# A sequence layer and an expert layer on one core: the same pieces of work, issued in another order

## The chip, the cores and the metric

The kernel runs on one core of a Trainium2 chip. The core has five engines that each take their own instructions strictly in the order in which the program issued them: TensorE (PE in the profile, with PEld for its weight loads), VectorE (DVE), ScalarE (ACT), GpSimd (POOL) and SyncE (SP, whose queue starts nearly all transfers). An instruction whose inputs are not there yet holds up everything behind it on its engine. The metric is the device time of one execution in microseconds (us); lower is better.

## The reference

Two residual layers run one behind the other, on 2048 positions of 512 channels, in float32:

```python
x = A_u                                  # 1 x 2048 x 512
h = x + S4D(layernorm(x))                # long convolution, one kernel of 2048 taps a channel
h2 = h + PEER(layernorm(h))              # 32 heads, each picks one of 256 experts

# S4D: 128 complex modes a channel
dt = exp(log_dt); A = -exp(log_A_real) + 1j * A_imag; C = (C_real + 1j * C_imag) * dt
K = 2 * Re(sum over the modes of C * exp(A * dt * position))       # 512 x 2048
y = irfft(rfft(u) * rfft(K)) + u * D_skip

# PEER: K = 1, so the softmax over the chosen ones is 1
s1 = q1 . k1 (16 scores), s2 = q2 . k2 (16 scores) for each position and head
expert = 16 * argmax(s1) + argmax(s2)
out = sum over the heads of gelu(xf . u[expert]) * v[expert]
```

## The kernel before, in words

**How the order is made.** The function does not issue instructions while it walks through the computation. It builds a `Plan`: `plan.add(engine, cost, fn, r=, w=, t=, ...)` records a piece of work as a closure, with the keys that it reads and writes, and numbers the pieces 0 to 1727 as they are added. At the end of the function `plan.run(ORDER)` calls the closures in the order of a table of 1728 numbers written at the top of the file; it only asserts that each piece's predecessors have run. A closure issues one instruction or many. So the table alone decides which instruction stands behind which on every engine, and in which order the transfers stand in SP's queue. Tiles come from small rings of buffers, and the first writer of a tile waits until the readers of the tile that had the buffer before are through: two buffers each for the tables `mg`, `pg` and `gf`, seven PSUM banks shared by most of the first phase, two and four PSUM tiles in the second, two for the raw weights `wq`.

**First phase, the convolution.** The 512 channels are treated as four blocks of 128 (the digit behind u, k, U, T, ia in the names), and the taps of each channel are produced by 32 *tables* (tab0 to tab31, eight for each block), 16 channels a table.
- The parameters are loaded and worked up once by ACT and DVE: decays `E0` (for tables 0 to 15) and `e1` (for tables 16 to 31, stored to DRAM and read back later) by 11 exponentials each in `decays` (L373), a root (L354), an arctangent (L355), the phase tables `RS0` and `A0` on DVE (L315 to L342, L364).
- A table: POOL makes the phases `pg` (L557) and the magnitudes `mg` (L588, its tails L594) out of the powers `TS` (L570 to L581) and the steps `PS` (L538 to L550); ACT takes sines and cosines (L644, L645, L647); DVE multiplies them (L651 to L664) into `gf` and `mg`; PE sums over the modes with 64 small matmuls into `kps` (L690), from which `k` is copied.
- Eight groups of weights w0 to w7 are folded from the query weights `wq` and the expert keys on PE (L828, L836) with ACT copies between (L832, L840) and stored to `w_d` (L844). They fill gaps of the first phase.
- The input is loaded twice, once for the statistics of the layernorm (`x`, L273; DVE statistics L232, PE sums L242 and L255, ACT root L262), once for the data (`xs`, L502; normalised on DVE at L505 and L508).
- The transform: stage 1 on PE (`s1u`, `s1k`, L471), ACT copies (L474), stage 2 (`s2yu`, `s2yk`, L488), the product of the spectra on DVE (L732 to L735, for block 3 with POOL's L743), the first stage back (`ia`, L764), copies to `T` (L772, L777), stores to `t_d` in DRAM (L789).

**Second phase, the experts.** The folded weights come back as `w_q` (L921), split into `w_hi` (ACT, L924) and `w_lo` (DVE, L925). Eight blocks of 256 positions follow, each as: the last stage back (`ib`, L1036) and the residual `h` on DVE (L1043), the layernorm's mean and centred values (PE L1093 and L1105, DVE L1073 and L1080, ACT L1076 and L1083), the variance (POOL L1060, PE L1124, ACT root L1128), scores `sc` (L1150), `xu` (L1157), the top of each head (DVE `mx` L1176, `eq` L1181, `kq` L1186; POOL `ks` L1192 and L1194; DVE `ei` L1199, `ix` L1202), the gelu (ACT L1206), the gather as a one-hot product (PE `ta` L1227, `ixt` L1242, `bc` L1258; ACT L1231, L1246, L1262; DVE compares `oh` L1280; PE `cnt` L1290; DVE `actT` L1299, ACT `whi` L1302, DVE `wlo` L1305), the sum over the experts (PE `o` L1327, for the last block L1324) and the residual (DVE `ob` L1332, store L1337). The last block is cut into two halves of 128 positions.

Of the kernel before, what the change touches and what calls it, by code (L numbers as in the profile page):

```python
# [27 lines left out]
def view(t, off, dims):  # L28
# [6 lines left out]
    16, 0, 2, 1, 17, 18, 4, 23, 80, 3, 5, 9, 7, 24, 65, 19, 26, 20, 180, 21, 22, 10, 34, 6, 183, 35, 36, 197, 29, 185,  # L35
    28, 58, 25, 31, 37, 39, 70, 40, 75, 41, 247, 32, 60, 30, 66, 67, 143, 983, 113, 12, 68, 244, 118, 42, 38, 44, 86,
    33, 61, 91, 114, 117, 120, 101, 43, 107, 119, 150, 11, 46, 27, 45, 53, 71, 47, 54, 76, 988, 77, 78, 48, 63, 55, 184,
    72, 73, 181, 74, 79, 87, 88, 81, 69, 82, 83, 92, 93, 84, 182, 198, 94, 187, 49, 50, 51, 189, 52, 62, 188, 96, 89,
    186, 190, 90, 191, 102, 103, 104, 196, 984, 248, 192, 193, 194, 56, 57, 64, 85, 199, 200, 993, 214, 105, 201, 202,
    985, 95, 195, 59, 215, 203, 245, 986, 97, 98, 8, 204, 99, 205, 100, 106, 108, 109, 110, 217, 206, 218, 216, 121,  # L40
    219, 220, 207, 221, 222, 223, 14, 994, 995, 127, 987, 224, 226, 229, 989, 990, 13, 126, 227, 231, 136, 208, 230,
    999, 123, 991, 992, 228, 232, 125, 209, 111, 1004, 225, 233, 1000, 234, 1009, 235, 1001, 236, 1002, 1003, 996, 1005,
    246, 997, 1006, 1007, 251, 253, 128, 998, 124, 1008, 255, 389, 237, 238, 257, 122, 210, 211, 115, 1014, 212, 213,
    15, 239, 116, 129, 249, 1010, 1020, 252, 250, 130, 1011, 1012, 1015, 254, 112, 131, 260, 263, 132, 133, 1013, 265,
    1025, 258, 1016, 1017, 242, 261, 256, 240, 134, 151, 1018, 262, 266, 267, 241, 269, 259, 135, 137, 138, 139, 141,
    264, 243, 278, 281, 140, 283, 152, 155, 142, 157, 270, 268, 386, 279, 280, 285, 156, 144, 282, 153, 154, 271, 1021,
    287, 1022, 1026, 1027, 290, 145, 284, 272, 293, 148, 286, 1028, 146, 149, 349, 1029, 158, 273, 295, 1023, 147, 297,
# [1401 lines left out]
```

## Time and profile before

| what | us |
|---|---|
| runs of the kernel before | 504.03, 503.99, 502.99 (median 503.99) |
| span of the profiled execution, first to last instruction | 503.2 |
| time of the profiled execution beside its span | not recorded apart; the three runs lie -0.2 to +0.8 about the span |
| PE busy, of the span | 449.0 (89%) |
| DVE busy | 407.8 (81%) |
| POOL busy | 325.5 (65%) |
| ACT busy | 298.3 (59%) |
| mean granted TensorE clock | 0.986 |

A row of the timeline reads: start, duration, engine, line, operation, output and inputs by the program's names, shapes, count; in square brackets the idle time of the engine just before the row, and what ended it. A row of the windows gives one stretch of the span: for each engine its busy time with the number of instructions in brackets, then the granted clock, the share of the 16 DMA engines, and what they moved. The profile's line numbers are those of the kernel before; in the kernel after each line stands one lower, since the table takes one line of text more.

### The profile page before, as it was taken

Reading aid. Unit: us, or ns where it says so; the run is one execution under the profiler, and the core shown is the slowest. Engines: PE = TensorE matmul, PEld = TensorE weight load, DVE = VectorE, ACT = ScalarE, POOL = GpSimd, SP = SyncE. Lnnn points to the kernel's source line nnn. Section 1 sums busy time; section 2 is a strip of 40 time slices with the busy share of each in tenths; the row PEclk is TensorE's granted clock in tenths of the full one; section 3 lists DMA queues with packets and bytes.
Section 4 is the critical chain, followed back from the end, with each engine's and each line's share of the span. In section 5 each row is a group of like instructions: output and inputs, shape, how many; then the busy total and the mean of one; then the engine's idle time right before and its main releaser. Section 6 shows DMA issues by size and latency. Waiting matters only on the chain.

```text
span 503.2 us, 16702 instructions
## 1 busy us (share of the span) xinstructions
PE 449.0 (89%) x7206; PEld 390.3 (78%) x7206; DVE 407.8 (81%) x708; ACT 298.3 (59%) x594; POOL 325.5 (65%) x344
## 2 busy tenths in 40 slices
PE   0266879999998999999998889999999999999985
PEld 0144568888997999889997787877878888787874
DVE  5998998899968998899745574888979686978984
ACT  4867799967987588967965362644043430416230
POOL 4989989999999999997824303572163516536130
PEclk9998799999999999999999899999999999999999
DMA  8959474234033300631017689310171311010012
GB/s 253 403 198 381 143 288 148 66 86 179 2 111 124 85 3 1 212 126 45 1 61 259 200 275 283 127 61 1 57 227 55 109 63 43 1 44 0 1 68 62
DMA packets 27362, 61.05 MB, mean 121 GB/s; under 512 B 7028, under 2 KB 14456, under 8 KB 26136
## 3 DMA queue, kind: packets, MB, share of 16 engines
q1 hardware_dynamic: 27136, 59.85, 34.9%
q8 instruction: 57, 0.93, 0.7%
q10 hardware_dynamic: 152, 0.13, 0.1%
q14 instruction: 17, 0.14, 0.1%
HBM read 46.08 MB, written 13.89 MB: 119 GB/s over the span
## 4 chain that ended last, share of the span: by engine, by line
PE 50%; DVE 22%; ACT 10%; POOL 10%; issue 4%; DMA 3%; SPq 1%; ACTq 0%; DVEq 0%; POOLq 0%
PE sc L1150 12%; PE ia L764 9%; DVE oh L1280 5%; PE s2yk L488 3%; PE xu L1157 3%; PE kps L690 3%; PE s2yu L488 3%; POOL pg L557 3%; PE s1u L471 3%; DVE st L232 2%; PE o L1327 2%; PE ib L1036 2%; PE cnt L1290 2%; ACT t L645 2%; POOL mg L594 2%
## 5 line engine op out<-in xcount | busy, mean ns | idle before, releaser
L557 POOL TENSOR_TENSOR pg<-PS 128x1024 int32<-128x1024 int32 x32 | 68.8, 2150 | 0.5
L588 POOL TENSOR_TENSOR mg<-TS 128x1024 f32<-128x1024 f32 x32 | 62.6, 1958 | 7.2 <-PE kps L690 4.5
L1280 DVE TENSOR_SCALAR oh<-idxb,ec_s 128x2048 bf16<-128x2048 bf16 (+1 forms) x72 | 50.3, 757 | 6.8 <-ACT idxb L1262 6.8
L764 PE MATMUL ia<-ca_s,U 128*128 128x128 f32 x256 | 50.6, 280 | 0.4 <-POOL U L743 0.4
L1060 POOL TENSOR_TENSOR vs<-hc 128x256 f32<-128x256 f32 x8 | 7.0, 872 | 62.6 <-ACT hc L1083 62.6
L1192 POOL TENSOR_TENSOR ks<-kq 128x512 f32<-128x512 bf16 x16 | 17.2, 1078 | 45.9 <-DVE kq L1186 44.8
L645 ACT ACTIVATE t<-t,halfpi 128x512 f32<-128x512 f32 x64 | 42.4, 662 | 2.1
L1150 PE MATMUL sc<-w_hi,hhi 128*128 128x480 f32 x128 | 42.4, 412 | 0.0
L644 ACT ACTIVATE t<-pg 128x512 f32<-128x512 int32 x64 | 38.9, 609 | 3.2 <-DVE gf L652 2.2
L764 PEld LDWEIGHTS ia<-ca_s,U 128*128 128x128 f32 x256 | 39.8, 196 | 0.6 <-POOL U L743 0.6
L647 ACT ACTIVATE t<-pg 128x512 f32<-128x512 int32 x64 | 38.2, 608 | 2.8 <-POOL pg L557 1.5
L764 PE MATMUL ia<-ca_s,yk 128*128 128x128 f32 x192 | 38.1, 280 | 0.4 <-DVE mg L664 0.4
L1150 PE MATMUL sc<-w_lo,hhi 128*128 128x480 f32 x128 | 38.4, 380 | 0.0
L1150 PE MATMUL sc<-w_hi,hlo 128*128 128x480 f32 x128 | 38.3, 380 | 0.0
L594 POOL TENSOR_TENSOR mg<-TS 128x512 f32<-128x512 f32 x32 | 37.4, 1170 | 0.4
L690 PE MATMUL kps<-mg 128*32 128x64 f32 x1024 | 34.0, 230 | 3.8 <-DVE mg L664 2.2
L488 PE MATMUL s2yk<-yk,c_s 128*128 128x128 f32 x256 | 34.7, 282 | 1.1 <-ACT yk L474 0.7
L471 PE MATMUL s1u<-c_s,xs 128*64 128x128 f32 x512 | 33.3, 277 | 2.5 <-DVE xs L508 1.6
L690 PE MATMUL kps<-gf 128*32 128x64 f32 x1024 | 33.7, 229 | 1.8 <-issue 1.8
L488 PEld LDWEIGHTS s2yk<-yk,c_s 128*128 128x128 f32 x256 | 30.6, 191 | 4.2 <-issue 1.4
L488 PE MATMUL s2yu<-yu,c_s 128*128 128x128 f32 x256 | 32.6, 279 | 0.3
L471 PEld LDWEIGHTS s1u<-c_s,xs 128*64 128x64 f32 x512 | 27.6, 137 | 5.4 <-DVE xs L508 1.7
(198 smaller groups left out, 1377.5 us busy)
## 6 DMA issues: line engine op xcount, KB each, us to landing
wq<-wq SPq DMA_DIRECT2D x25, 512.0 KB, 4.5
t_d<-T SPq DMA_DIRECT2D x24, 256.0 KB, 3.4
Tb<-t_d SPq DMA_DIRECT2D x8, 768.0 KB, 6.0
x<-xa SPq DMA_DIRECT2D x8, 512.0 KB, 5.6
xs<-xb SPq DMA_DIRECT2D x16, 256.0 KB, 5.3
xt<-xt SPq DMA_DIRECT2D x8, 512.0 KB, 4.8
out<-ob SPq DMA_DIRECT2D x7, 512.0 KB, 3.0
c_s<-wq SPq DMA_DIRECT2D x4, 512.0 KB, 8.3
```

Of the source, the lines that this page charges most:

```text
L471: T.matmul(ps[64 * k:64 * k + 64, g, :], lhs8(4 * n + g), c1_s[:, k], start=True, stop=True)
L488: T.matmul(ps[:, k, :], c2_s[:, kk, :], y[:, :, kk, :], start=True, stop=True)
L557: G.tensor_tensor(view(pg, 0, [[32, 2 * NC], [8, 4], [1, 8]]), view(t["PS"], 1024 + off, [[1, 2 * NC], [128, 4], [0, 8]]), view(t["PS"], 8 ...
L588: G.tensor_tensor(view(mg, 0, [[96, NC], [8, 8], [1, 8]]), view(ts, 512 + 8 * o, [[8, NC], [1, 8], [0, 8]]), view(ts, 8 * o, [[8, NC], [0, ...
L594: G.tensor_tensor(view(mg, 64, [[96, NC], [8, 4], [1, 8]]), view(ts, 1536 + o, [[1, NC], [64, 4], [0, 8]]), view(ts, 1024 + 8 * o, [[8, NC ...
L644: A.activation(p, pg[:, :, k], AF.Abs)
L645: A.activation(p, p, AF.Sin, scale=-SINSCALE, bias=halfpi)
L647: A.activation(p, pg[:, :, k], AF.Sin, scale=SINSCALE)
L690: T.matmul(kps[32 * q:32 * q + 32, 2 * g + h, :], m[:, d, 64:96], m[:, d, 0:64], start=(e == 0), stop=(e == 1))
L764: T.matmul(ps[:, g, :], t[:, 4 * n + g].rearrange("p a b -> p (a b)"), ca_s[:, s, :], start=(s == 0), stop=(s == 1))
L1150: T.matmul(ps[:, 512 * h:512 * h + 480], t[x_][:, q, ts], I[w_][:, q, 480 * h:480 * h + 480], start=(q == 0 and x_ == w_), stop=(q == 3 an ...
L1280: V.tensor_scalar(oh[:, :, 0:ln], t["idxb"][:, :, sl], S["ec"][:, 4 * e + j:4 * e + j + 1], None, op0=ALU.is_equal)
```

## The change

Only the table `ORDER` is another: the same 1728 numbers in another order. No piece of work, no tile, no ring, no shape and no engine of a piece differs. The first rows of the diff show how it looks:

```diff
@@ -32,87 +32,88 @@
 ORDER = (
-    16, 0, 2, 1, 17, 18, 4, 23, 80, 3, 5, 9, 7, 24, 65, 19, 26, 20, 180, 21, 22, 10, 34, 6, 183, 35, 36, 197, 29, 185,
...
```

The order differs nearly everywhere, on every engine. ACT gets four instructions more, 562 rows where there were 558: table loads, since the activation functions alternate more often (one pair around `e1`, one pair in the second phase). All other engines issue the same instructions. Three places follow in rows of the issue order; a name with a number behind it is one tile, and x11 stands for eleven instructions in a row.

**ACT in the first part of the program, before.** The eleven exponentials of `e1` stand between the two parts of `E0` and ahead of the arctangent (L355), on which the phases of the first table hang.

```order
L373 ACTIVATE E0_116<-pb_98 128x64 x11
L351 ACTIVATE par2_101<-pa_97 128x64
L353 ACTIVATE pb_98<-pa_97 128x64
L373 ACTIVATE e1_104<-pb_98 128x256 x11
L352 ACTIVATE pa_97<-pa_97 128x64
L373 ACTIVATE E0_116<-pb_98 128x192 x11
```

After, at the same place:

```order
L374 ACTIVATE E0_116<-pb_98 128x64 x11
L352 ACTIVATE par2_101<-pa_97 128x64
L354 ACTIVATE pb_98<-pa_97 128x64
L353 ACTIVATE pa_97<-pa_97 128x64
L374 ACTIVATE E0_116<-pb_98 128x192 x11
```

and 61 rows further down, behind the sines of table 3:

```order
L646 ACTIVATE t11_3_612<-t11_3_612,halfpi_62 128x512
L841 COPY wh2_551<-wps10_592 128x120
L833 COPY wt13_646<-wps13_633 128x128
L374 ACT_TABLE_LOAD
L374 ACTIVATE e1_104<-pb_98 128x256 x11
L833 COPY wt12_734<-wps12_693 128x128
L699 COPY k0_1_759<-kps0_1_648 128x512
L841 COPY wh3_771<-wps12_693 128x120
L648 ACT_TABLE_LOAD
L648 ACTIVATE t00_4_799<-pg4_773 128x512
```

What moved: `e1` out of the way of the arctangent, to a place where it costs a change of table there and back. On DVE, the statistics of the layernorm (L232), of which 24 stood before the first table's products, now all stand behind them; on PE the sums of the tables (`kps`) stand further back among the other matmuls throughout the first phase. SP issues `ka` and `kb` before three of the five parameters, and the last two of the eight loads of `x` behind the second store of folded weights.

**DVE at the turn from the first phase to the second, before.** The last copies of the first phase (`T3`) are followed by two splits of the query weights, and these by the residual of the first block, from which the mean is taken.

```order
L777 COPY T3_4229<-ia3_2_4319 64x64x4 x2
L777 COPY T3_4229<-ia3_4_4337 64x64x4 x2
L925 TENSOR_TENSOR w_lo_4193<-w_q1_4309,w_hi_4192 128x960
L925 TENSOR_TENSOR w_lo_4193<-w_q0_4312,w_hi_4192 128x960
L1043 TENSOR_TENSOR h0_4418<-ib0_0_4366,xt0_4316 128x4x128
L1043 TENSOR_TENSOR h0_4418<-ib0_1_4383,xt0_4316 128x4x128
```

After:

```order
L778 COPY T3_4257<-ia3_6_4298 64x64x4 x2
L778 COPY T3_4257<-ia3_5_4307 64x64x4 x2
L926 TENSOR_TENSOR w_lo_4196<-w_q0_4281,w_hi_4195 128x960
L948 CAST ident_b_4197<-ident_60 128x128
L949 MEMSET ones_d_4198 128x128
L1044 TENSOR_TENSOR h0_4415<-ib0_1_4363,xt0_4361 128x4x128
L1044 TENSOR_TENSOR h0_4415<-ib0_0_4380,xt0_4361 128x4x128
```

What moved: one of the two splits, that of `w_q1`, stands behind the centring of the first block now. A little earlier, in SP's queue, three of the last four loads of `wq` stand ahead of the stores of `T2` (L789) and the fourth between their two halves; before, all four stood behind all eight stores. On PE two of the four folds of w7 (`wps28`, `wps29`) now stand ahead of the last stage 2 of block 3 (`s2yk3`), and the other two ahead of its fifth and seventh part, each behind the wait for its own load; before, the four were spread from its fifth part to its end.

**DVE at the end, before.** `oh65` to `oh71` and `oh64` are the compares of the second half of the last block, `oh60` the last of the first half.

```order
L1280 TENSOR_SCALAR oh60_7147<-idxb7_6999,ec_s_4198 128x8x128
L1299 TENSOR_TENSOR actT7_7080<-cnt7_0_7105,actT7_7080 128x2x128
L1280 TENSOR_SCALAR oh65_7182<-idxb7_6999,ec_s_4198 128x8x128
L1280 TENSOR_SCALAR oh67_7184<-idxb7_6999,ec_s_4198 128x8x128
L1280 TENSOR_SCALAR oh66_7186<-idxb7_6999,ec_s_4198 128x8x128
L1280 TENSOR_SCALAR oh64_7188<-idxb7_6999,ec_s_4198 128x8x128
```

After:

```order
L1281 TENSOR_SCALAR oh60_7145<-idxb7_7006,ec_s_4201 128x8x128
L1281 TENSOR_SCALAR oh65_7148<-idxb7_7006,ec_s_4201 128x8x128
L1281 TENSOR_SCALAR oh64_7186<-idxb7_7006,ec_s_4201 128x8x128
L1281 TENSOR_SCALAR oh67_7188<-idxb7_7006,ec_s_4201 128x8x128
L1281 TENSOR_SCALAR oh66_7190<-idxb7_7006,ec_s_4201 128x8x128
L1300 TENSOR_TENSOR actT7_7079<-cnt7_0_7093,actT7_7079 128x2x128
```

What moved: four compares of the second half ahead of the product of the first half. On PE, both broadcasts `bc` of the second half and half of the first half's `cnt` stand ahead of its twelve `xu` matmuls (before: `xu` first), and the first half's `o` stands between the two halves of the second `cnt` (before: ahead of both).

162 rows, old and new, of the table ORDER are left out of this document.

## The prediction, as put on record before the changed kernel ran

> **What bounds the kernel now.** I read the page's first part, then the windows, then the timeline where the windows show TensorE idle.
>
> ```profile
> PE 449.0 (89%) x7206; PEld 390.3 (78%) x7206; DVE 407.8 (81%) x708; ACT 298.3 (59%) x594; POOL 325.5 (65%) x344
> ```
>
> PE is idle for 503.2 - 449.0 = 54.2 us; no order of the same matmuls can win more than that. Where it is idle, the windows say:
>
> ```profile
> 0.00:20.00 20.00, 2.05 (x29) 1.37 (x33) 13.87 (x41) 13.40 (x47) 12.27 (x24) 1.00 0.89 307
> 20.00:40.00 20.00, 11.82 (x195) 7.53 (x187) 19.08 (x51) 12.17 (x31) 17.54 (x22) 1.00 0.73 272
> 40.00:60.00 20.00, 13.86 (x314) 10.31 (x314) 18.66 (x61) 16.13 (x37) 19.61 (x18) 0.74 0.78 284
> 60.00:80.00 20.00, 16.66 (x417) 13.82 (x420) 18.99 (x35) 18.58 (x39) 18.12 (x16) 1.00 0.56 199
> 70.00:255.00 185.00, 180.28 (x3396) 166.54 (x3397) 162.74 (x268) 152.85 (x292) 173.66 (x158) 1.00 0.26 85
> 262.00:282.00 20.00, 16.47 (x267) 14.22 (x264) 11.99 (x20) 10.84 (x24) 10.11 (x8) 1.00 0.67 226
> 340.00:360.00 20.00, 20.00 (x195) 16.37 (x193) 18.07 (x28) 5.35 (x11) 3.72 (x4) 1.00 0.01 2
> 480.00:503.20 23.20, 16.09 (x270) 13.71 (x262) 14.85 (x29) 6.24 (x12) 2.97 (x4) 1.00 0.21 71
> ```
>
> The columns behind the length are PE, PEld, DVE, ACT and POOL. In the first 80 us PE is idle for 35.6 us while DVE is full from about 6 us on; from 70 to 255 PE is idle for only 4.7 us, with POOL close behind it (173.7 of 185); at the turn of the phases it loses 3.5 us in 20; in the second phase nothing; at the end 7.1. So a new order can win at the start (by getting DVE's work done sooner), at the turn, and at the end. In between it can only lose, or win the 4.7.
>
> **The start.** PE becomes full when the first stage 1 of the input can run, and this hangs on the last statistic of the layernorm on DVE:
>
> ```profile
> 11.49 3.48 ACT L373 ACTIVATE e<-pb 128x256 f32<-128x256 f32 x11 [1.11 <-DVE pb L359]
> 25.30 0.24 ACT L355 ACTIVATE pa<-pa 128x64 f32<-128x64 f32 x1
> 29.32 2.13 POOL L557 TENSOR_TENSOR pg<-PS 128x1024 int32<-128x1024 int32 x1
> 6.20:67.90 61.70, 33.20 (x664) 23.42 (x664) 57.93 (x162) 46.69 (x125) 56.25 (x60) 0.92 0.81 296
> 47.87 0.87 DVE L232 BATCH_NORM_STATS2 st<-x 128x6 f32<-128x128 f32 x4 [1.34 <-DMA x<-xa]
> 67.92 1.97 PE L471 MATMUL s1u<-c_s,xs 128*64 128x128 f32 x32 [1.58 <-DVE xs L508]
> ```
>
> Taking `e1` (3.48 us) from ACT's path, and 24 statistics from DVE's (four take 0.87, so 5.2), lets the arctangent at 25.30 and the first phases at 29.32 come some 3.5 to 5 us sooner, with the first tables behind them. But s1u does not wait for tables. It waits for DVE, and DVE does the same instructions ahead of it: of the 61.7 us up to s1u it is busy for 57.9. The most that an order can win is the 3.8 idle, of which 1.34 is the wait for x; the two last loads of x now stand behind one store more, so this wait can also grow. I take -0.3, with -3.8 and +2 as bounds. The two table loads around `e1`, with `e1` itself, are 3.5 + 2.6 = 6.1 us on ACT at its new place behind table 3. ACT has room there: 3.9 us idle in 40:60, and at least 3.5 by which its sines start sooner, 7.4 together. Uncovered the 6.1 would fall on the table chain.
>
> ```profile
> 18.88 0.57 ACT L352 ACTIVATE pa<-pa 128x448 f32<-128x448 f32 x1
> 19.48 1.28 ACT L354 ACT_TABLE_LOAD   x1
> 20.77 0.21 ACT L354 ACTIVATE par<-par 128x64 f32<-128x64 f32 x1
> ```
>
> A switch costs 1.28 here, since the instruction ahead ends at 19.45 and the next starts at 20.77. The Trainium skill speaks against this part of the change more strongly: "ScalarE: Activation LUTs", section "What ACT_TABLE_LOAD costs", counts a drain of about 1.38 us on top of 1.28 for every switch, 2.66 in all. By the page the pair and `e1` would be 3.5 + 5.3 = 8.8 us, 1.4 more than the room, and the forecast at most 1.4 us later. The trace does not agree: its row shows no drain, and the sum goes by the row.
>
> While s1u waits, PE works off one fold of weights more than before (34 matmul groups of L828 ahead of it, not 32), which is gone from the full stretch:
>
> ```profile
> 60.49 0.43 PE L828 MATMUL wps<-wq,ka_s 128*32 128x128 f32 x8 [0.42 <-DVE gf L652]
> 60.73 0.40 PE L828 MATMUL wps<-wq,kb_s 128*32 128x128 f32 x8
> 61.52 0.33 PE L836 MATMUL wps<-ident,wt 128*128 128x128 f32 x1 [0.39 <-ACT wt L832]
> ```
>
> 0.64 from the first start to the second end, and 0.33 less overlap: -0.9, or 0 if PE had a hole for it later anyway.
>
> **The full stretch.** Matmuls are the same. The order puts the sums of the tables (kps) later among them, so PE should wait less for DVE's tables, but POOL gets its two `mg` buffers back later:
>
> ```profile
> L588 POOL TENSOR_TENSOR mg<-TS 128x1024 f32<-128x1024 f32 x32 | 62.6, 1958 | 7.2 <-PE kps L690 4.5
> L690 PE MATMUL kps<-mg 128*32 128x64 f32 x1024 | 34.0, 230 | 3.8 <-DVE mg L664 2.2
> 156.88 0.26 PE L690 MATMUL kps<-gf 128*32 128x64 f32 x4 [1.78 <-issue]
> 254.08 1.16 POOL L594 TENSOR_TENSOR mg<-TS 128x512 f32<-128x512 f32 x1
> 262.07 0.32 PE L690 MATMUL kps<-mg 128*32 128x64 f32 x8
> ```
>
> POOL is through with table 31 at 255.24, and PE takes up its sum at 262.07; what ACT and DVE do between is 2 to 3 us, so some 4 us of delay on POOL stay unseen. I take 0. Bounds: -3.8, PE's waits for tables gone, and +5, a delay of 9 on POOL.
>
> **The turn.** Up to the first `ia` the pace is DVE's, then POOL's:
>
> ```profile
> 269.31 0.69 DVE L732 TENSOR_TENSOR yu<-s2yk,U 128x512 f32<-128x512 f32 x1 [5.28 <-ACT ki L739]
> 276.87 0.69 DVE L732 TENSOR_TENSOR yu<-s2yk,U 128x512 f32<-128x512 f32 x1 [0.36 <-ACT ki L739]
> 281.84 0.71 PE L764 MATMUL ia<-ca_s,U 128*128 128x128 f32 x2 [0.36 <-POOL U L743]
> ```
>
> One fold and two transposes more stand ahead of stage 2, about 1.0 us by the rows above; the new place of the four wq loads in SP's queue removes the late wq, for DVE 0.36. Together +0.6, between 0 and +1.3.
>
> Behind the last copy of T, two w_lo hold up `h`, the mean and so the scores:
>
> ```profile
> 299.51 2.23 DVE L925 TENSOR_TENSOR w_lo<-w_q,w_hi 128x960 fp32r<-128x960 f32 x2
> 301.77 1.29 DVE L1043 TENSOR_TENSOR h<-ib,xt 128x512 f32<-128x512 f32 x2
> 303.71 0.69 DVE L1073 TENSOR_TENSOR hc<-h,mean 128x512 f32<-128x512 f32 x1 [0.65 <-PE mean L1093]
> 305.21 0.68 DVE L1080 TENSOR_TENSOR hlo<-hc,hhi 128x512 fp32r<-128x512 f32 x1
> ```
>
> One leaves: -1.1; two small casts that came before now stand there: +0.4. One half's hlo now precedes the other half's hc, 0.6 sooner. Late next is the second half, which the first scores cover. Taken: -1.2; bounds -2 (the scores of the half that is ready start at once) and 0 (w_hi or x is late instead).
>
> **The second phase.** PE is full in 340:360, and no work changes. The two table loads more, 2.6 us, lie on an ACT that is busy for 5.35 of 20. 0, between -1.5 and +1.5.
>
> **The end.** DVE waits, then has eight compares left:
>
> ```profile
> 492.13 0.42 DVE L1299 TENSOR_TENSOR actT<-cnt,actT 128x256 f32<-128x256 f32 x1 [2.37 <-PE ta L1227]
> 492.47 3.25 DVE L1280 TENSOR_SCALAR oh<-idxb,ec_s 128x1024 bf16<-128x1024 bf16 x8
> 488.25 1.63 PE xu L1157 x12
> 496.97 2.07 PE o L1324 x16
> 499.06 0.69 DVE L1332 TENSOR_TENSOR ob<-o,h 128x512 f32<-128x512 f32 x1 [1.55 <-PE o L1324]
> ```
>
> Four compares, 1.6 us, move into the 2.37, which their inputs allow because `bc` no longer queues behind xu's 1.63. The last compare is then done about 1.6 sooner. But the first half's `o`, 2.07 long, now stands between the halves of the last `cnt` and ends later than the last compare; this gives some 0.3 back. -1.3, between -1.9 and 0.
>
> Sum: -0.3 - 0.9 + 0 + 0.6 - 1.2 + 0 - 1.3 = -3.1 against the span of 503.2: 500.1. The median of the runs lies 0.8 above that span, so **about 500.9 us**.
>
> **Rivals.** A measurement of this kernel tells 0.2% (1.0 us) from no change.
>
> *No change.* The gains at turn and end are 2.5 us together; a POOL delay of 6 (2 beyond the cover) cancels most. For it: the stretch in which PE has no slack is most of the span, and its order is shuffled throughout. Time: 503.2 to 504.5.
>
> *POOL becomes the bound: slower.* Place: POOL's L588 in the later tables. A kps that is late by one table on PE makes POOL stand; a table is 2.15 + 1.96 + 1.17 = 5.3 us of POOL by its rows (first row below; the others are quoted above and here). Two such stalls, 10.6, less the cover of 4, push the sum of table 31, the turn and all behind by 6.6; with -3.1 this is +3.5, about 507.5. It decides as soon as POOL's delay exceeds 4 + 3.1 = 7.1 us. For it: POOL has 11.3 us of idle time in 185. Against it: earlier tables at the start give it a lead of 3.5 to 5.
>
> ```profile
> L557 POOL TENSOR_TENSOR pg<-PS 128x1024 int32<-128x1024 int32 x32 | 68.8, 2150 | 0.5
> L594 POOL TENSOR_TENSOR mg<-TS 128x512 f32<-128x512 f32 x32 | 37.4, 1170 | 0.4
> ```
>
> *The start pays.* DVE's 3.8 idle vanishes (3.5 beyond what I took) and PE's 1.78 of "issue" does not recur: 500.9 - 5.3 = 495.6. For it: tables are ready earlier, so DVE always has work. Against it: x's transfers are not earlier.
>
> **Chances.** Forecast (a gain of 1 to 5 us) 0.46, no change 0.18, POOL bound or another loss 0.27, start pays 0.09. So faster 0.55, same 0.18, slower 0.27. The forecast's own range is 499 to 503; with the other cases 496 to 507, which leaves out the far halves of the last two.
>
> **What would show it.** Right: s1u starts at 66 to 68.5; POOL's table 31 ends by 259; `ia` of block 3 starts at 280 to 282; the first sc is 1 to 2 us closer to the last `ia`; DVE's wait before the last-but-one actT product is under 1 us, and the last o ends 1 us sooner after the last sc. Wrong: L588's idle time above 12 us in all; s1u after 70; a new idle window of PE between 320 and 460.

## The result: slower, 522.5 us against 503.5

| | before | after |
|---|---|---|
| median of the runs, us | 503.49 (502.76 to 504.03, 4 runs) | 522.50 (520.48 to 523.15, 3 runs) |
| after / before | | 1.035, 95% interval 1.030 to 1.041 (1.038 by the two medians) |
| span of the profiled execution, us | 503.2 | 518.4 (of a run of 520.48) |
| mean granted TensorE clock | 0.986 | 0.963 |

The new order costs 19.0 us, where 3 us of gain were forecast. The medians here and below leave out two runs in the chip's slower state, one of the changed kernel (529.65) and one of the second phase alone (521.64); with them the loss reads 19.3 and the second phase 514.2, as two expectations below have it. The two profiles show 15.2 of the 19.0. That of after is of its shortest run, 2.0 us below the median. That of before has a span of 503.2, and in all runs whose span is on record the time lies 1.7 to 3.4 us above the span: by this estimate that execution took 504.9 us or more, 1.4 or more above its median. The two together make up 3.4 or more of the 3.8. First the stretches between five milestones, by the windows view, before and then after. The milestones are the first `s1u`, the first `ia` of block 3, the first score, the last `o` of the last block but one, and the end; the columns behind the length are PE, PEld, DVE, ACT, POOL, granted clock, DMA share, GB/s.

```profile
0.00:67.90 67.90, 33.20 (x664) 23.42 (x664) 58.52 (x164) 48.40 (x128) 57.15 (x69) 0.92 0.80 286
67.90:281.10 213.20, 205.07 (x3857) 188.28 (x3858) 178.88 (x292) 169.62 (x328) 185.43 (x167) 1.00 0.30 100
281.10:307.00 25.90, 23.14 (x401) 21.84 (x400) 16.61 (x32) 11.93 (x24) 0.68 (x1) 0.93 0.80 246
307.00:487.40 180.40, 177.85 (x2109) 148.89 (x2103) 146.14 (x205) 65.82 (x109) 82.23 (x109) 1.00 0.21 71
487.40:503.20 15.80, 9.70 (x185) 7.89 (x183) 7.63 (x19) 2.54 (x6) 0.00 (x0) 1.00 0.22 69
```

```profile
0.00:72.00 72.00, 36.94 (x680) 25.90 (x681) 60.21 (x165) 51.02 (x129) 58.48 (x72) 0.80 0.71 253
72.00:283.00 211.00, 205.63 (x3851) 188.76 (x3843) 177.68 (x290) 170.07 (x330) 183.62 (x162) 1.00 0.33 109
283.00:311.00 28.00, 23.51 (x401) 22.18 (x401) 16.40 (x33) 11.45 (x23) 1.26 (x1) 0.94 0.72 224
311.00:504.00 193.00, 182.97 (x2101) 148.98 (x2101) 158.31 (x206) 68.71 (x112) 90.31 (x109) 0.99 0.20 64
504.00:518.40 14.40, 9.52 (x185) 8.00 (x185) 7.66 (x18) 2.53 (x6) 0.00 (x0) 0.97 0.24 75
```

Start +4.1, full stretch -2.2, turn +2.1, second phase +12.6, end -1.4: together +15.2. The work is the same, and yet DVE is busy 12.2 us longer in the second phase and POOL 8.1. PE's share of the 12.6 is in two parts: it is idle for 10.0 us where it was idle for 2.6, and it is busy for 5.1 us more with the same matmuls (182.97 against 177.85). The largest loss lies where PE was full and where the forecast had put nothing.

**The start, after.** The timeline of ACT, and then of DVE and PE, around the new place of `e1`:

```profile
52.52 1.28 ACT L374 ACT_TABLE_LOAD   x1
53.81 3.48 ACT L374 ACTIVATE e<-pb 128x256 f32<-128x256 f32 x11
...
58.53 1.28 ACT L648 ACT_TABLE_LOAD   x1
59.83 1.12 ACT L648 ACTIVATE t<-pg 128x512 f32<-128x512 int32 x2
```

```profile
41.47 0.69 DVE L665 TENSOR_TENSOR mg<-mg,t 128x512 f32<-128x512 f32 x1 [1.67 <-ACT t L646]
...
58.38 0.17 DVE L703 TENSOR_TENSOR k<-kps,D 128x8 f32<-128x8 f32 x1 [0.27 <-ACT k L699]
...
61.05 0.69 DVE L656 TENSOR_TENSOR gf<-mg,t 128x512 f32<-128x512 f32 x1 [0.95 <-ACT t L648]
61.65 1.64 DVE L233 BATCH_NORM_STATS2 st<-x 128x6 f32<-128x128 f32 x8
...
65.27 0.23 DVE L246 COPY pc<-mu 128x64 f32<-128x64 f32 x1 [0.80 <-PE mu L243]
...
72.25 4.42 PE L472 MATMUL s1u<-c_s,xs 128*64 128x128 f32 x64
```

The eleven exponentials and the two loads keep the sines off ACT from 52.52 to 59.83. DVE's product waits for a sine behind them (0.95), with the last eight statistics behind that product. The waits of DVE from 6.5 us up to its last statistic sum to 4.6 us, where they were 1.5 before, and some 1.6 us of other DVE work now stands ahead of it too; a first wait for the parameters is 0.6 shorter. So the last statistic ends 4.0 us later and s1u starts 4.3 later. Behind `e1` DVE waits only twice, 0.27 for the copy of `k` and 0.95 for the sine: 1.2 of the 4.6. The 1.67 at 41.47, ahead of `e1`, and 1.7 of waits for parameters in the first 20 us are not its doing.

**POOL in the full stretch, after**: its group of the magnitudes on the page, and the end of its table 31 on the timeline (255.24 before):

```profile
L589 POOL TENSOR_TENSOR mg<-TS 128x1024 f32<-128x1024 f32 x32 | 62.5, 1955 | 13.5 <-PE kps L691 9.8
```

```profile
260.03 1.16 POOL L595 TENSOR_TENSOR mg<-TS 128x512 f32<-128x512 f32 x1
```

POOL stands 13.5 us, 6.3 more than before, and ends 6 us later. The first `ia` of block 3 is less late than that, 2.1 (283.20 against 281.08).

**The second phase, after.** The waits of PE from 311 to 500 (before, 311 to 500 again, in the second fence: us in total, times, the longest):

```profile
PE ixt L1243 <- DVE ix L1203: 4.1, 6, 1.3
PE cnt L1291 <- DVE oh L1281: 2.2, 4, 0.9
```

```profile
PE cnt L1290 <- DVE oh L1280: 1.2, 3, 0.6
...
PE ixt L1242 <- DVE ix L1202: 0.4, 1, 0.4
```

The groups by line of the same operations, after and then before (busy us, mean ns of one):

```profile
L1281 DVE TENSOR_SCALAR oh<-idxb,ec_s 128x2048 bf16<-128x2048 bf16 (+1 forms) x72 | 53.9, 802 | 0.7 <-ACT idxb L1263 0.7
...
L1203 DVE SCALAR_TENSOR_TENSOR ix<-ei 128x32 bf16<-128x32 int32 x16 | 8.3, 519 | 0.6
...
L1193 POOL TENSOR_TENSOR ks<-kq 128x512 f32<-128x512 bf16 x16 | 19.3, 1204 | 50.8 <-DVE kq L1187 45.2
L1195 POOL TENSOR_TENSOR ks<-ks 128x256 f32<-128x256 f32 (+2 forms) x48 | 33.6, 700 | 3.8
```

```profile
L1280 DVE TENSOR_SCALAR oh<-idxb,ec_s 128x2048 bf16<-128x2048 bf16 (+1 forms) x72 | 50.3, 757 | 6.8 <-ACT idxb L1262 6.8
...
L1202 DVE SCALAR_TENSOR_TENSOR ix<-ei 128x32 bf16<-128x32 int32 x16 | 6.1, 381 | 0.6
...
L1194 POOL TENSOR_TENSOR ks<-ks 128x256 f32<-128x256 f32 (+2 forms) x48 | 28.9, 602 | 3.8
L1192 POOL TENSOR_TENSOR ks<-kq 128x512 f32<-128x512 bf16 x16 | 17.2, 1078 | 45.9 <-DVE kq L1186 44.8 <-DVE rstd L1134 1.1
```

PE waits for the index `ix` and the compares `oh`, and both take longer on average, as do POOL's key sums `ks`, on which the index hangs: a whole sum takes POOL (17.2 + 28.9) / 16 = 2.9 us before and (19.3 + 33.6) / 16 = 3.3 after. Two instances of one instruction in the timeline of after show the pattern: POOL's row lies over the first and not over the second (the POOL row ahead of it ends at 336.58).

```profile
346.18 1.01 DVE L1203 SCALAR_TENSOR_TENSOR ix<-ei 128x32 bf16<-128x32 int32 x1
346.09 1.05 POOL L1193 TENSOR_TENSOR ks<-kq 128x512 f32<-128x512 bf16 x1 [1.57 <-DVE kq L1187]
...
336.70 0.19 DVE L1203 SCALAR_TENSOR_TENSOR ix<-ei 128x32 bf16<-128x32 int32 x1
```

For each DVE row of the second phase I took its excess over the shortest row of its line. In the rows that overlap a POOL row this sums to 10.8 us before (310 to 480) and 22.0 us after (310 to 496); in the rows that overlap none to 1.4 and 1.1. The overlap itself grew from 61 to 72 us. Of the 22.0 the compares make 8.3, `ix` 5.2 and `ei` 3.8. The price of one row is the same in both orders: a compare of 128x2048 takes 0.74 us on average alone and 0.99 beside POOL. But 32 of them lie beside POOL now, where 18 did, and 9 of the 16 `ix` are stretched, where 6 were. In both traces each stretched `ix` starts 0.03 to 0.15 us behind the start of a row of POOL and ends within 0.06 us behind the end of that row, as at 346.18 above. Seven of the nine after lie so beside the layernorm's sums on POOL (L1061 to L1063) and two beside the key sums.

**The end, after.** By the timeline of DVE the wait of 2.37 before the last-but-one product is 0.21 now, and a wait of 1.61 stands ahead of the last one:

```profile
508.15 0.42 DVE L1300 TENSOR_TENSOR actT<-cnt,actT 128x256 f32<-128x256 f32 x1 [0.21 <-PE cnt L1291]
...
511.76 0.42 DVE L1300 TENSOR_TENSOR actT<-cnt,actT 128x256 f32<-128x256 f32 x1 [1.61 <-PE cnt L1291]
```

### The profile page after: what moved, and what is told of

It reads as the page before. It is cut to its first block, busy times and chain, and to the rows that moved or that the text cites. A ratio compares the mean times of both kernels' runs of the same rounds, so it can differ in the third digit from the quotient of the medians.

```text
span 518.4 us, 16691 instructions
## 1 busy us (share of the span) xinstructions
PE 458.6 (88%) x7206; PEld 393.8 (76%) x7206; DVE 420.3 (81%) x708; ACT 303.8 (59%) x598; POOL 333.7 (64%) x344
## 4 chain that ended last, share of the span: by engine, by line
PE 59%; DVE 18%; POOL 8%; ACT 5%; DMA 4%; issue 4%; SPq 1%; POOLq 0%; DVEq 0%; ACTq 0%
PE ia L765 10%; PE sc L1151 9%; PE kps L691 5%; PE s1u L472 5%; PE s1k L472 5%; PE s2yk L489 5%; PE s2yu L489 4%; DVE oh L1281 4%; PE cnt L1291 3%; PE ib L1037 2%; PE o L1328 2%; PE xu L1158 2%; POOL pg L558 2%; DVE mx L1177 2%; POOL mg L589 1%
## 5 line engine op out<-in xcount | busy, mean ns | idle before, releaser
L589 POOL TENSOR_TENSOR mg<-TS 128x1024 f32<-128x1024 f32 x32 | 62.5, 1955 | 13.5 <-PE kps L691 9.8
L1281 DVE TENSOR_SCALAR oh<-idxb,ec_s 128x2048 bf16<-128x2048 bf16 (+1 forms) x72 | 53.9, 802 | 0.7 <-ACT idxb L1263 0.7
L1193 POOL TENSOR_TENSOR ks<-kq 128x512 f32<-128x512 bf16 x16 | 19.3, 1204 | 50.8 <-DVE kq L1187 45.2
L1195 POOL TENSOR_TENSOR ks<-ks 128x256 f32<-128x256 f32 (+2 forms) x48 | 33.6, 700 | 3.8
L1061 POOL TENSOR_TENSOR vs<-hc 128x256 f32<-128x256 f32 x8 | 6.5, 818 | 42.3 <-ACT hc L1084 42.3
L472 PE MATMUL s1k<-c_s,k 128*64 128x128 f32 x512 | 31.9, 280 | 1.3 <-issue 0.8
```

Source lines behind the costliest of these rows:

```text
L472: T.matmul(ps[64 * k:64 * k + 64, g, :], lhs8(4 * n + g), c1_s[:, k], start=True, stop=True)
L589: G.tensor_tensor(view(mg, 0, [[96, NC], [8, 8], [1, 8]]), view(ts, 512 + 8 * o, [[8, NC], [1, 8], [0, 8]]), view(ts, 8 * o, [[8, NC], [0, ...
L1281: V.tensor_scalar(oh[:, :, 0:ln], t["idxb"][:, :, sl], S["ec"][:, 4 * e + j:4 * e + j + 1], None, op0=ALU.is_equal)
```

## The experiments

In the diffs A is the table after and B the table before; "A[: place]" are A's numbers ahead of that place, "rest of B" the numbers left over, in B's order. A kernel of two such pieces is a legal order in itself, with a seam at which an engine may find its next work unusually early or late.

| kernel | us | before, us | ratio (95%) |
|---|---|---|---|
| first phase as after | 511.61 | 504.05 | 1.017 (1.011 to 1.022) |
| second phase as after | 512.94 | 504.05 | 1.018 (1.013 to 1.024) |
| the same once more | 515.66 | 504.00 | 1.022 (1.015 to 1.029) |
| start alone | 513.21 | 504.05 | 1.017 (1.013 to 1.022) |
| full stretch and turn alone | 513.12 | 504.19 | 1.019 (1.014 to 1.023) |
| turn alone | 504.05 | 504.19 | 1.001 (0.998 to 1.003) |
| end alone | 502.82 | 504.05 | 0.998 (0.996 to 1.001) |
| only `e1` late | 508.22 | 504.96 | 1.007 (1.004 to 1.011) |
| `e1` and statistics late | 511.80 | 504.96 | 1.014 (1.011 to 1.017) |
| after, `e1` put back | 527.44 | 504.18 | 1.044 (1.039 to 1.050) |
| second phase, `ixt`, `cnt` later | 530.33 | 504.19 | 1.053 (1.049 to 1.057) |
| more POOL work | 530.56 | 504.19 | 1.054 (1.050 to 1.057) |
| shorter key sum, before | 503.52 | 504.96 | 0.997 (0.994 to 1.000) |
| shorter key sum, second phase | 512.00 | 504.96 | 1.013 (1.009 to 1.017) |
| little POOL, before | 500.01 | 504.18 | 0.990 (0.985 to 0.995) |
| little POOL, second phase | 505.69 | 504.18 | 1.000 (0.998 to 1.003) |
| little POOL, after | 510.47 | 504.00 | 1.014 (1.005 to 1.022) |

### Which part costs what

```diff
-ORDER = B
+ORDER = A[: first score] + rest of B     # first phase as after
```

> The order of the changed kernel up to the first scores of block 0, and from there the pieces that are left in the order of the kernel before. Theory (two places lose: the start, and the select work of the second phase, which the order puts on TensorE before DVE has its inputs ready): the loss of the first phase alone, about 3.9 us by the traces at the first score, so about 507.5 us. Rival of the prediction (POOL gets its buffers back late and all behind it moves): nearly the whole loss, 518 to 522.

```diff
-ORDER = B
+ORDER = B[: first score] + rest of A     # second phase as after
```

> The order of the kernel before up to the first score of block 0, and from there the order of the changed kernel. Theory (two places lose): the second phase loses 12.6 us and its end gains 1.3, so about 515 us. Rival (POOL's buffers in the first phase): no loss here, 502 to 504.

```diff
-ORDER = B
+ORDER = A[: first s1u] + rest of B       # start alone
```

> The order of the changed kernel up to the first stage 1 of the input, the rest as before. Theory (the start itself loses: the last statistic on DVE comes 4 us late): the first s1u starts at about 72 instead of 68 and 2 to 4.5 us of it stay to the end, 505.5 to 508. Rival (the start is neutral and the order of the stretch behind it loses): 502.5 to 504.5.

```diff
-ORDER = B
+ORDER = B[: the last block's last scores] + rest of A     # end alone
```

> The order of the kernel before up to the last xu but one of the last block, and from there the order of the changed kernel. Prediction's term for the end: -1.3 us, so 502.2. Rival (the compares that move forward only change where DVE waits): 503.5.

First phase +7.6, more than the 3.9 expected of it and far less than the rival's whole loss; second phase +8.9, and +11.7 in the repeat below. Together they make 16.5 to 19.3 of the 19.0, so the seam at the first score is a clean one within what the runs can tell. The start alone already gives +9.2, more than expected and more than the whole first phase. Its seam adds a wait, in PE's timeline:

```profile
80.82 0.66 PE L828 MATMUL wps<-wq,ka_s 128*32 128x128 f32 x8 [2.79 <-DMA wq<-wq]
```

A fold taken up early waits there for a load that before's order sends late; in the two whole orders the longest such wait behind the start is 1.3 (before) and 0.6. The end alone gains 1.2 in the medians, and the interval just touches no change; its trace shows the predicted rows (0.13 before the last-but-one product, 1.61 before the last), and from the end of the last `o` of the last block but one it takes 14.5 us, as the changed kernel does, where before took 15.8.

```diff
-ORDER = B
+ORDER = B[: first s1u] + A's remaining numbers up to the first score + rest of B     # full stretch and turn
```

> The start (up to the first stage 1 of the input) in the order of the kernel before, then the changed order up to the first score of block 0, then again the kernel before. Theory (the first phase loses at its start): 503 to 505, within 1 us of the kernel before. Rival (POOL's buffers come back late in the full stretch): 507 or more, with over 12 us of idle time ahead of POOL's magnitudes.

```diff
-ORDER = B
+ORDER = B[: last ia of block 3] + A's remaining numbers up to the first score + rest of B     # turn alone
```

> Only the turn, from behind the last ia of block 3 to the first score of block 0, in the changed order. Prediction's term: -1.2 (one w_lo less ahead of h), so 502.8. Rival from the trace of the changed kernel (the mean waits behind the next block's ib on TensorE, and a hole of 2 us within ib in which TensorE waits for nothing shown): 504 to 505.5.

The stretch has a seam of its own (a fold that waits 6.18 us for `wq` at 72.87, ahead of s1u), so its +8.9 cannot be read as the price of the stretch: start and stretch are +9.2 and +8.9 apart and +7.6 together. The orders of neighbouring stretches are made for each other. By its number the rival came, and POOL stands 15.8 us ahead of its magnitudes; but from s1u to the first `ia` of block 3 this trace takes 210.9 us, as the changed kernel does (211.0), and before took 213.2. So the late buffers are not what costs.

The turn alone is neutral in the medians. In its trace the first of the two splits starts at 298.28 and the first score at 305.11, 6.83 us; in the profile of before it was 299.51 to 307.03, 7.52; in the changed kernel it is 302.23 to 310.9, 8.7. The 0.7 between the first two are no gain of the order: the profile of before has a hole of 0.76 there, told of below. From the end of the last copy of `T3` to the first score the turn alone takes 6.86 us; of the thirteen traces with the old order of the turn, nine take 6.49 to 6.52, and before, with 7.55, is the longest. So the new order of the turn wins nothing by itself. The timelines of DVE and PE there, after:

```profile
306.43 0.69 DVE L1074 TENSOR_TENSOR hc<-h,mean 128x512 f32<-128x512 f32 x1 [1.44 <-PE mean L1094]
...
310.68 0.25 PE L1037 MATMUL ib<-cb,Tb 128*32 128x64 f32 x3 [2.00 <-issue]
```

`h` is there sooner after the copies, but the mean comes late on PE, and then PE stands for 2.00 us inside a burst of small matmuls and waits for nothing that the profile shows. Before, the like hole is 0.76. It is 2.27 with the first phase as after, 3.30 with the full stretch and turn alone, and the turn alone has none, nor have the start alone and the second phase alone: so it goes with the new order of the full stretch. What in it makes the hole stays open.

### The start: is it `e1`?

```diff
 (B, order of ACT and SP)
-..., 29, 185, 28, 58, 25, 31, 37, ...
+..., 29, 185, 28, 25, 31, 37, ..., 234, 1009, 235, 58, 59, 1001, ...     # 58: e1, 59: its store
```

> The kernel before with one edit: the eleven exponentials of e1 stand behind the sines of table 3, as in the changed kernel, with the two table loads that this takes. Prediction's view (they are covered, and the arctangent comes 3.5 us sooner): s1u at 67 to 68.5, time 502.5 to 504.5. Rival from the changed kernel's trace (6.05 us on ACT between the tables hold up table 4 and the last statistics): s1u 1 to 2 us later, 505 to 506.

```diff
 (as above, and on DVE)
-..., 983, 113, 12, 68, 244, 118, 42, ..., 91, 114, 117, 120, 101, 43, 107, 119, 150, ...
+..., 192, 193, 194, 113, 118, 114, 117, 120, 119, 56, 57, ...     # the statistics behind table 0's products
```

> The same, and the 24 first statistics of the layernorm stand behind the products of table 0 on DVE, as in the changed kernel. Theory (the statistics filled DVE's waits among the parameters; moved, the waits stay idle and the last statistic comes late): s1u 2 to 4 us later than the 67.9 of the kernel before, time 505.5 to 508. Rival (DVE has the same work ahead of s1u, so the order doesn't matter): s1u within 1 us, 503 to 505.

`e1` alone, moved to behind the sines of table 3 in an otherwise unchanged order, costs 3.3 us and puts s1u at 73.00, 5.1 later. With the statistics it is 6.8 us and 76.45. Both are more than any side had expected. The timelines of ACT, PE and DVE with `e1` alone, in order of time, and of DVE with both:

```profile
53.27 3.48 ACT L373 ACTIVATE e<-pb 128x256 f32<-128x256 f32 x11
...
56.95 0.69 PE L836 MATMUL wps<-ident,wt 128*128 128x128 f32 x2 [5.17 <-ACT wt L832]
...
62.77 0.59 ACT L698 COPY k<-kps 128x512 f32<-128x512 f32 x1
...
63.39 0.17 DVE L702 TENSOR_TENSOR k<-kps,D 128x8 f32<-128x8 f32 x1 [5.67 <-ACT k L698]
```

```profile
66.84 0.17 DVE L702 TENSOR_TENSOR k<-kps,D 128x8 f32<-128x8 f32 x1 [6.87 <-ACT k L698]
```

An addition of 0.17 us on DVE waits 5.67 us for a copy that stands behind `e1` on ACT, and the last statistics stand behind that addition. PE's folds wait as well, 5.17, for ACT's copy of the fold before. The forecast weighed the 6.1 us of the moved block against ACT's idle time and the sooner sines. The arctangent does start sooner in the changed kernel (21.06 for 25.30) and with both edits (22.68), but not with `e1` alone (25.48); and it does not help, because what waits is not a table. In the changed kernel itself, with another order on DVE, the same addition waits 0.27 (above): there `e1` is a small part of the delay.

```diff
 (A, order of ACT)
-..., 80, 66, 36, 37, 39, 40, ..., 1006, 225, 1007, 58, 1000, ...
+..., 80, 66, 36, 58, 37, 39, 40, ..., 1006, 225, 1007, 1000, ...
```

> The changed kernel with one edit undone: the exponentials of e1 stand between the two parts of E0 again, with no table loads of their own. Theory (e1 behind table 3 costs 3 us at the end, as in the kernel before with that edit alone): 518 to 520.5. Rival (in the changed order the arctangent needs e1 out of its way): 522 or more.

This expectation fell, and the rival's number came: with `e1` back at its old place the changed order is not faster but 4 to 5 us slower still (527.44 against 522.50; s1u at 74.35). Its timeline of DVE shows where, and behind it stands the same place before:

```profile
17.64 0.23 DVE L361 TENSOR_TENSOR par<-par,pa 128x64 f32<-128x64 f32 x1 [3.77 <-ACT par L351]
```

```profile
17.28 1.64 DVE L232 BATCH_NORM_STATS2 st<-x 128x6 f32<-128x128 f32 x8
18.83 0.22 DVE L361 TENSOR_TENSOR par<-par,pa 128x64 f32<-128x64 f32 x1
```

Before, statistics stand on DVE where the wait is now. They stand elsewhere in the new order, so `e1` there stalls DVE openly. So once the statistics have moved, `e1` has to move too; the reverse does not hold, since the late `e1` costs 3.3 with the statistics at their old place and 6.8 without. Neither place is good: late, `e1` blocks the copies; early, it blocks parameters.

### The second phase: what makes it 9 to 12 us longer?

The first idea was that PE reaches `ixt` and `cnt` too early in the new order.

```diff
-ORDER = (second phase as after)
+ORDER = (the same, 18 of 21 pieces of ixt and cnt moved back on PE, by up to one group of scores)
```

> The second phase in the changed order as in the run with that part alone (514.2), but on TensorE the transposes of the indices (ixt) and the cnt products of blocks 0 to 6 stand later, where the dependences allow it, by up to one group of scores (0.3 to 2.3 us by the trace's rows); 18 of 21 are moved. Theory (TensorE stalls because they stand too early for DVE): the waits at ixt and cnt fall below 2 us and the time to 505 to 509. Rival (DVE, slowed beside POOL, sets the pace whatever TensorE's order): 512 or more, and the stalls reappear at other rows of TensorE.

It fell, and the rival came: 15 to 17 us slower than without the move. DVE's product now waits for `cnt` (waits of DVE, 306 to 500), and the chain of each block goes through it. Not all of the loss is waiting, though. From the first score to the end the trace takes 223.1 us, 16.2 more than the second phase as after in its repeat (206.9): 6.0 of these are idle time of PE, and 10.2 are longer busy time of the same matmuls, at a granted clock of 0.95 over this stretch against 1.00.

```profile
DVE actT L1299 <- PE cnt L1290: 16.9, 6, 7.0
```

The second idea was contention: DVE slowed by POOL. To price it, POOL got work whose result nobody reads:

```diff
+    dum = con.tile([P, 256], F32, name="dum")
+    G.memset(dum, 0.0)
...
             for w in (4, 2, 1):
                 G.tensor_tensor(kt_[:, :, 0:w], kt_[:, :, 0:w], kt_[:, :, w:2 * w], op=ALU.add)
+            for _ in range(4):
+                G.tensor_tensor(dum, dum, dum, op=ALU.add)
```

> The kernel before, with four additions of 128x256 on GpSimd (about 0.7 us each, their result read by nobody) behind each of the 16 sums of keys in the second phase. Theory (DVE's compares stretch while GpSimd runs): the mean of the compares rises from 0.76 to 0.8 or more and the time by 2 to 6 us, though GpSimd is idle half of the phase. Rival (GpSimd matters by the latency of its own chain only): within 1 us of 504.

47.5 us of such work cost 26.4, far above the 2 to 6 that were expected; the mean of the compares rose to 0.815, as expected. PE's longest waits (306 to 520) were

```profile
PE mean L1107 <- POOL hs L1064: 8.9, 3, 4.4
PE ixt L1246 <- DVE ix L1206: 5.9, 4, 2.7
PE cnt L1294 <- DVE oh L1284: 4.1, 2, 2.2
```

The lower two are the waits of the changed kernel, and the excess of DVE's rows beside POOL is the same, 21.8 us. But the uppermost is something else: POOL's queue delays its own sums. So this run shows that POOL's work can bring out these two waits, not what they cost in the changed order. For that, work was taken away instead, in two steps.

```diff
-            for w in (4, 2, 1):
+            for w in (1,):
                 G.tensor_tensor(kt_[:, :, 0:w], kt_[:, :, 0:w], kt_[:, :, w:2 * w], op=ALU.add)
```

> The kernel before without two of the three halvings in GpSimd's sum of keys (so the chosen experts are wrong): GpSimd has about 1.5 us less work for each of 16 groups. A control for the next run. Both theories: TensorE is full here, so 500 to 504.

> The same halvings left out where the second phase has the changed order. Theory (the changed order loses there since GpSimd's sums run beside DVE's compares, both stretch, and TensorE waits for them): the loss against the control falls from 10 to 5 us or less. Rival (the order of TensorE and DVE among themselves costs the 10): still 8 to 11 above the control.

With two of three halvings left out the second phase still costs 8.5 us over its control, as the rival said, where it was 8.9 with the whole sums (11.7 in the second phase taken once more). But the excess beside POOL fell little (18.8 us here, 8.5 in the control), since most of the stretched `ix` lie beside the layernorm's sums, which this edit leaves. So it mostly shortens the key sum, by 1.4 us each, and says that this is worth 0.4 to 3.2 us.

```diff
-            G.tensor_tensor(s_, s_, q[:, 2], op=ALU.add)
-            G.tensor_tensor(s_, s_, q[:, 3], op=ALU.add)
...
-            G.tensor_tensor(kt_, d["kq"][:, :, 0:8], d["kq"][:, :, 7:15], op=ALU.add)
-            for w in (4, 2, 1):
-                G.tensor_tensor(kt_[:, :, 0:w], kt_[:, :, 0:w], kt_[:, :, w:2 * w], op=ALU.add)
+            G.tensor_tensor(kt_[:, :, 0:1], d["kq"][:, :, 0:1], d["kq"][:, :, 7:8], op=ALU.add)
```

> The kernel before with most of GpSimd's work in the second phase left out (two of three additions of each sum of squares and of channels, and the sum of keys reduced to one addition of 128x64; mean, variance and chosen experts are wrong by that). A control for the next run: DVE's rows are stretched beside GpSimd by 10.8 us in the kernel before, here by less than 4; 499 to 504.

> The same left out where the second phase has the changed order. Theory (the 10 us are DVE's rows stretched beside GpSimd, 22 us against 11, which TensorE then waits for): the stretch falls below 6 us and the loss against the control to 4 us or less. Rival (the order of DVE and TensorE among themselves): the loss against the control stays 7 to 11, with DVE's stretch gone.

> The whole changed order, with the same work of GpSimd left out of the second phase as in its two relatives before (of the key sums and of the layernorm's sums of squares; so the experts picked and the variance are not the reference's). The changed order costs 19.3 us with that work. Its pair in the order before costs 500.0 without it. If contention of VectorE with GpSimd makes 4.5 to 7.4 us of the loss, as the pair without that work left between its two readings (4.5 by the medians, 7.4 by the profiles from the first score on), this kernel takes 500.0 + 12 to 15 = 512 to 515 us. If the order alone costs it all, 500.0 + 19 = 519. If most of the second phase's loss in the changed order is contention, 500.0 + 8 = 508. In the trace, from the first score to the end: 207.5 us in the changed kernel, 196.2 before, 192.2 before without the work; contention says 196 to 200 here, order alone 203.

> The order before up to the first score, the changed order behind it, taken once more with the whole work of GpSimd: for the trace from the first score to the end, which the earlier one does not give undisturbed. If the loss of the second phase is a property of the order, that stretch takes 206 to 208 us as in the whole change (196.2 before), and the time is again 10 +- 2 us above before. If what comes ahead of the first score (a later or earlier arrival of blocks 1 to 7) makes part of it, the stretch is under 204.

The control without most of POOL's work takes 500.01, as expected. With the second phase as after it takes 505.69, so the loss falls from 8.9 (11.7 in the repeat) to 5.7, between what theory (4 or less) and rival (7 to 11) had said; with the whole table after it takes 510.47, so the loss falls from 19.0 to 10.5, by 8.5 us, beyond what I had expected (512 to 515). The traces, from the first score to the end: 196.2 before, 207.5 after, 207.0 in the second phase taken once more, as expected of a loss that is the order's own; without POOL's work 192.2, 195.8 with the table after and 196.2 with the second phase alone. So +11.3 and +10.8 become +3.6 and +3.9. Some 7 of the 11 us go away with POOL's work by the traces, 3 to 6 by the medians of the second phase alone. The waits of PE (311 to 492) and the groups of `oh` and `ix` with the table after and little POOL:

```profile
PE ib L1036 <- issue: 2.0, 1, 2.0
PE cnt L1286 <- issue: 1.1, 1, 1.1
```

```profile
L1276 DVE TENSOR_SCALAR oh<-idxb,ec_s 128x2048 bf16<-128x2048 bf16 (+1 forms) x72 | 47.3, 712 | 2.0 <-ACT idxb L1258 1.8
...
L1198 DVE SCALAR_TENSOR_TENSOR ix<-ei 128x32 bf16<-128x32 int32 x16 | 3.5, 217 | 0.5
```

The waits for `ix` and `oh` are gone, `oh` is back from 802 to 712 ns and `ix` from 519 to 217, and the excess beside POOL is 3.4 us. So by the traces the second phase's loss hangs on POOL's work for about two thirds. How it does so is only half settled, because these kernels take several things away together: DVE's rows are no longer stretched, and POOL's own sums are shorter, the key sum by 2.8 us (3.3 to 0.5) and the layernorm's by two additions of three. The halvings took 1.4 off each key sum for 0.4 to 3.2 us; doubled, that would be 1 to 6 of the 7. PE's idle time from the first score to the end scatters less: the new order adds 6.3 us to it in the changed kernel and 6.7 in the repeat, 5.2 with the halvings left out, and 1.7 without most of POOL's work, in both kernels. By estimate from these, if the gain is in proportion, the shorter key sum takes 2 to 3 of the 4.6 to 5.0 us of idle time that go with POOL's work, and the rest is left for the stretched rows and the layernorm's sums. That DVE is stretched beside POOL, and twice as much as before, is shown; its own share of the 7 is open. The 3.6 to 3.9 us that stay without POOL's work belong to the order itself, and no single wait in those traces carries them: 1.7 are idle time of PE, 1.9 and 2.2 are longer busy time for the same matmuls.

## Why the prediction was wrong, step by step

Two terms failed, and the larger is the second phase, put at nothing because PE is full there; the other is the start.

- **"s1u does not wait for tables. It waits for DVE, and DVE does the same instructions ahead of it", -0.3.** Wrong, +4.3, outside its bounds (-3.8 to +2); the mark "s1u after 70" came. Same instructions do not make the same time: DVE's rows hang on ACT, whose rows come in their own order, so DVE waits 4.6 us ahead of its last statistic where it waited 1.5, and it does 1.6 us of other work first. The step that failed is the bound: what DVE waited before is not the most that an order can change.
- **"ACT has room there: ... 7.4 together."** Wrong as an argument: `e1` alone, in the old order, puts s1u 5.1 later. Idle time of an engine in a window of 20 us is not room for a block of 6.1 us in one piece; what counts is the first row behind the block, there a copy of `k`, and who waits for it. In the changed kernel this step is the smaller part of the start's loss, 1.2 us of DVE's waits.
- **The table load, 1.28 a switch.** Right. After, the load ends at 53.80 and the exponentials start at 53.81. The Trainium skill, "ScalarE: Activation LUTs", section "What ACT_TABLE_LOAD costs", counts 2.66 with a drain; the new place again shows none. Later is what came, as by the page's figure, but not for a drain.
- **One fold more ahead of s1u, -0.9, and the full stretch, 0.** The stretch is 2.2 shorter, so the sign is right. It is the new order of the stretch that does it and not the late start: with the old order behind an s1u that is 5.1 or 8.5 late the stretch takes 212.8 and 213.1, before 213.2. That the fold is the cause was not shown, so the right sign may be luck.
- **The rival "POOL becomes the bound".** Its mark came (L589 idle above 12 us, table 31 after 259) and the sign was right, but it is not where the time went: `ia` of block 3 is 2.1 late, less than s1u was. What of it is POOL's own was not taken apart, since the stretch alone had a seam.
- **The turn, +0.6 and -1.2.** Wrong: 2.1 longer, of which 2.00 is a hole on PE that nothing in the profile explains. The gain of 1.2 did not come with the turn alone either, where the first score stands 9.6 us behind the last `ia` (9.5 before, 10.8 after). The profile from which the term was read holds a hole of 0.76 of its own in the last rows ahead of the first score, and none of the twelve other traces with the same order does.
- **The second phase, "PE is full in 340:360, and no work changes. ... 0, between -1.5 and +1.5."** Wrong, and by far the largest term: +12.6. That PE is full says that the old order hides all that DVE and POOL do, not that any order does. PE, idle for 2.6 us of that phase before (180.40 less 177.85), is idle for 10.0 now, and busy for 5.1 more. The term allowed for table loads alone; it had no price for DVE rows that come to lie beside POOL rows, though the page before had `ix` at 0.19 and at 1.02 us in two places.
- **The end, -1.3.** Right: -1.4 in the stretches, with the 2.37 gone and a wait for the second `cnt` in its place, as forecast; alone -1.2, not clear of the noise.

The range failed because its upper end was one mechanism on POOL (507.5), while two others came together, each worth more than its bounds. Small beside this: the 0.8 us added for the time beside the span compares one execution's span with other executions' times; where both are on record the difference is 1.7 to 3.4.

## What to carry to other kernels

When a hand-made order is changed, a block that moves is to be priced by the first instruction queued behind it on its engine and by who waits for that one on another engine; the idle share of a window says nothing of this. A full engine is not a safe one: what is hidden under it in the old order has to be found, row by row, and asked whether the new order still hides it, above all where VectorE rows come to lie beside GpSimd rows, whose longest and shortest instance tell the price. And since the parts of an order are made for each other, pieces put into the old order are to be read by their traces first: their sums held at one seam of two here. A row that a term is read from should be looked up in a second execution of the same order: the turn of the profile before was the longest of thirteen.

## What the runs showed of the hardware

- DVE's rows stretch beside POOL's, small ones by the largest factor: `ix` takes 0.19 us alone and up to 1.02 beside a key sum, in the kernel before, and 1.01 after. Each stretched `ix` of the two traces starts just behind a row of POOL and ends within 0.06 us behind its end, so it takes as long as what is left of that row. Not every row is hit: `mx`, `eq`, `h`, `ob` and `actT` keep their means within 0.01 us beside POOL, while the 128x2048 compare goes from 0.74 to 0.99, up to 1.54. Taking most of POOL's work away turns the mean of `oh` from 757 to 697 ns in the order before and from 802 to 712 after. The Trainium skill, "GPSIMD Engine Reference", section 1 ("Specifications"), says that POOL shares its SBUF interfaces with VectorE and names instructions in a two-port mode or with two SBUF inputs; the traces agree that there is contention. The page gives no size; here it is some 11 us of excess in the order before and 22 after.
- POOL is slowed as well: the halvings of the key sums take 602 ns on average before and 700 after, the same 48 instructions. Its addition of 128x64 takes 0.31 us with no row of DVE beside it and up to 0.83 beside a compare (after).
- The granted clock differs with the order: over the first 68 us it is 0.82 in the changed kernel, 0.82, 0.82 and 0.90 in the three others with the whole new start, and 0.90 to 0.95 in seven with the old one. In the second phase with `ixt` and `cnt` later it is 0.95, and 10.2 us of that kernel's loss are longer busy time of PE.
- PE can stand for 2.0 to 3.4 us inside a burst of small `ib` matmuls while the profile shows nothing that it waits for: in all five kernels with the new order of the full stretch (2.00, 2.00, 2.27, 3.30, 3.38), and for 0.76 at most with the old one.
